# Moving the first attention steps of batch 1 out of the first FFN tile of batch 0

## The chip, the core and the metric

The kernel runs on one core of a Trainium2 chip. The metric is the device time of one execution in microseconds (us). A core has TensorE for matrix products (PE; its weight loads are listed as PEld), VectorE (DVE), ScalarE (ACT), GpSimd (POOL) and SyncE (SP), which here issues the loads and stores. Each engine works through its own list of instructions in order and waits, where an instruction needs something, for the engine or the transfer that makes it.

## The reference

Eight batches, eight heads, 576 rows of q, k and v with 64 columns, and 32 pack rows p. Per batch and head two softmax attentions follow one another; then an FFN with a softplus between its layers.

```
def sm_attn(qq, kk, vv):
    s = scale * matmul(qq, kk.T)
    a = exp(s - max(s)); a = a / (sum(a) + 1e-9)
    return matmul(a, vv)
p_packed = sm_attn(p, k, v)
out = sm_attn(q, p_packed, p_packed)
x = out as (4608, 512)
h = x @ w_in                                   # 512 x 2048
g = maximum(h, 0) + log1p(exp(-abs(h)))
return g @ w_out                               # 2048 x 512
```

## The kernel before

**Tiles and slots.** The FFN runs over units (b, f): 8 batches of 576 rows times 16 tiles of 128 columns of the hidden layer. In the text a tile is one unit, counted within its batch, and `u` is its number over all batches. The second layer of a unit runs LAG = 2 units behind its first, so in unit u PE does, in this order: `gemm1` of u (12 matmuls, six for each of two halves of the 576 rows, into `ph_u_0` and `ph_u_1`), then four slots, t = 0 to 3, with three matmuls each into `acc_t` for unit u - 2, and every so often `make_m`, which prepares the weights of a later tile. All fp32 operands of the FFN are split in a high and a low part (`at_h`/`at_l`, `mh`/`ml`, `gh`/`gl`, `wo_h`/`wo_l`), hence three matmuls for each product.

**Softplus.** ACT takes Abs (L603), Exp (L605) and Ln (L606) of a `ph` pair into `e`; DVE adds max(h, 0) (L608) and splits the result into `gh` and `gl` (L595, L596). `ph` has two banks, so `ph_u_0` of the next tile has to wait for L608 on the half before. POOL keeps the last 64 rows (`rest`, L612).

**Attention folded in.** `make_m` multiplies the packed result `pt` with `w_in` into `psm`, so that the first layer needs only the second softmax (`at`). The attention of batch b + 1 is a generator, `attention_first` for batches 0 and 1. It yields after each of its 30 steps. The order of batch 1's steps on PE is: four transposes of k for head group 0 (`psT_k_0_0` to `psT_k_0_3`, copied by ACT to `T_k` at L269), scores, four transposes of k for group 1 with softmax in between, `psa` (transposed weights) and `psp` (times v, scaled by DVE into `pp` at L327), transposes of q, `psx` (pt), and the second scores and softmax, which end in `aT`. `weights(b + 1)` at the last tile of a batch turns `aT` into `at_h` (ACT, L526) and `at_l` (DVE, L527).

**When a step runs.** In every slot `due` grows by PACE = 0.56 (0.62 while b is 1), and one step is taken for each whole unit of it. `due` starts at 0 at each batch's first tile. So batch 1's first two steps fall into the slots of batch 0's tile 0, and its 30th into tile 13. At tile 15 whatever is left would be run at once; nothing is left.

**Weight conversion.** `w_in` and `w_out` come as 64-bit floats and are converted in 32 pieces by a second generator, `convert`: ACT makes `m` and `r` (L200, L204), DVE `t` (L206, L211), POOL adds them into `w_in_sb` or `r` (L219), and for `w_out` ACT and DVE split the sum (L238, L244). Most of it runs in batch 0's slots, at CONV = 1.6 steps for each slot. In batch 0 a `psm` pair serves two tiles and needs the columns of two pieces of `w_in`; it stands at the end of the slots two tiles ahead. So the last two pieces are needed ahead of tile 13, by the `psm` for tiles 14 and 15.

**Banks.** Everything of the attention and `psm` share two PSUM banks (`ps_m`, taken in turn). A tile that takes a bank waits until the reader of the tile before the last is done.

**Order.** PE's instructions run in the order of the code. The order on ACT, DVE, POOL and SP is set when the kernel is built, by a list scheduler that goes by priority and by what it takes to be ready; so moving a step in the code can also reorder the conversion and the softplus on these engines.

Of the kernel before, what the change touches and what calls it, by code (L numbers as in the profile page):

```python
# [26 lines left out]
def pack_attention_then_softplus_ffn(  # L27
# [27 lines left out]
    FIRST = 2  # L55
# [39 lines left out]
    def load_pack(bg, queues):  # L95

        t = cv.tile([PW, H, D], F32, tag="m", name=f"p_{bg}", bufs=1)
        for i in range(BG):
            queues[i % len(queues)].dma_start(
                t[i * J:(i + 1) * J], p[bg * BG + i].rearrange("h j d -> j h d")  # L100
            )
        return t

    def pack_transposed(bg, t):
        for o in range(0, H, HG):
            ps = bank(f"ppt_{bg}_{o}")
            for i in range(HG):
                nc.tensor.transpose(
                    ps[:D, i * PW:(i + 1) * PW], t[:, o + i, :], ident[:PW, :PW]
                )  # L110
            dst = pT[:, o:o + HG, :].rearrange("x h j -> x (h j)")
            nc.vector.tensor_copy(dst[:D], ps[:D, :HG * PW])
            nc.scalar.copy(dst[D:], ps[:D, :HG * PW])
# [402 lines left out]
    def attention(b):  # L516
        return attention_first(b) if b < FIRST else attention_next(b)

    def weights(b):

        at_h = work.tile([P, G, S], F32R, tag="at_h", name=f"at_h_{b}", bufs=1)
        at_l = work.tile([P, G, S], F32R, tag="at_l", name=f"at_l_{b}", bufs=1)
        res[b]["at"] = (at_h, at_l)
        for g in range(G):
            aT = res[b]["aT"][g]
            nc.scalar.copy(at_h[:, g, :], aT)  # L526
            nc.vector.tensor_tensor(  # L527
                at_l[:, g, :], aT, at_h[:, g, :].bitcast(F32), op=ALU.subtract
            )


    def m_cols(b):

        return MC if b else MC // 2
# [30 lines left out]
    def gemm1(b, f, res):  # L565

        n = m_cols(b)
        halves = res["m"][f * P // n]
        at_h, at_l = res["at"]
        phs = []  # L570
        for c in range(2):
            ph = ps_h.tile([P, 512], F32, tag="h", name=f"ph_{b}_{f}_{c}")
            phs.append(ph[:, :C])
            i = 0
            for g in range(G):
                mh, ml = halves[g * n // MC]
                o = g * n % MC + f * P % n
                ms = slice(o, o + P)
                cs = slice(c * C, (c + 1) * C)
                for x, y in ((mh, at_h), (mh, at_l), (ml, at_h)):  # L580
                    nc.tensor.matmul(  # L581
                        ph[:, :C], x[:, ms], y[:, g, cs],
                        start=(i == 0), stop=(i == 3 * G - 1),
                    )
                    i += 1
        return phs
# [11 lines left out]
    def softplus(b, f, hv, done):  # L598
        e = work.tile([P, S], F32, tag="e", name=f"e_{b}_{f}")
        es = [e[:, c * C:(c + 1) * C] for c in range(2)]  # L600
        spans = [e] if b == 0 else es
        for c in range(2):
            nc.scalar.activation(es[c], hv[c], AF.Abs)  # L603
            for x in spans[c:c + 1] if b else spans[:c]:
                nc.scalar.activation(x, x, AF.Exp, scale=-1.0)  # L605
                nc.scalar.activation(x, x, AF.Ln, bias=1.0)  # L606
        for c in range(2):
            nc.vector.scalar_tensor_tensor(es[c], hv[c], 0.0, es[c], op0=ALU.max, op1=ALU.add)  # L608
        yield
        yield  # L610
        r = (b % 2) * REST
        nc.gpsimd.tensor_copy(rest[:, rest_at(b, f), r:r + REST], e[:, NT * P:])  # L612
        yield
        done[b, f] = halves(f"{b}_{f}")
        split(*done[b, f], e[:, :NT * P])

    def gemm2_tile(acc, gh, gl, f, cs, first, last):
        for i, (x, y) in enumerate(((gh, wo_h), (gh, wo_l), (gl, wo_h))):
            nc.tensor.matmul(  # L619
                acc, x[:, cs], y[:, f, :],  # L620
                start=(first and i == 0), stop=(last and i == 2),
            )
# [13 lines left out]
    def store(acc, pieces, nm, t):  # L636
        if t % 2 == 0:
            half[:] = [cv.tile([P, 2, DM], F32, tag="x", name=f"o_{nm}", bufs=2)]
        o = half[0][:, t % 2, :]
        nc.vector.tensor_copy(o, acc)  # L640
        for row, b, col, n in pieces:
            while n:
                m, dst = rows(b, col, n)
                nc.sync.dma_start(dst, o[row:row + m, :])
                row, col, n = row + m, col + m, n - m

    def rests(b):


        fs = sorted(range(NF), key=lambda x: rest_at(b, x))  # L650
        gh, gl = halves(f"{b}_m")
        n = NT // 2
        for i in range(0, NF, n):
            o = rest_at(b, fs[i])
            c = i % NT * P
            cs = slice(c, c + n * P)
            split(gh[:, cs], gl[:, cs], rest[:, o:o + n, :].rearrange("x f j -> x (f j)"))
            if i == 0:
                yield
                am = ps_acc.tile([P, DM], F32, tag="acc", name=f"acc_{b}_m")  # L660
            for t in range(n):
                gemm2_tile(
                    am, gh, gl, fs[i + t], slice(c + t * P, c + (t + 1) * P),
                    i + t == 0, i + t == NF - 1,
                )
        store(am, [(0, b - 1, NT * P, REST), (REST, b, NT * P, REST)], f"{b}_m", NT)
        yield
# [7 lines left out]
    PACE = 0.56  # L675
    FRONT = 1000
    PACE_FIRST = 0.62
# [18 lines left out]
    due = 0.0  # L696
# [20 lines left out]
    ahead, chain, due = iter(()), iter(()), 0.0  # L717
    for u in range(len(units) + LAG):
        if u < len(units):
            b, f = units[u]  # L720
            if f == 0:
                if (b + 1) % BG == 0 and b + 1 < B:
                    pack_transposed((b + 1) // BG, pt)
                ahead = attention(b + 1) if b + 1 < B else iter(())
                due = 0.0
            chain = softplus(b, f, gemm1(b, f, res[b]), gs)
            next(chain)
            if f == NF - 1:
                if (b + 2) % BG == 0 and b + 2 < B:
                    pt = load_pack((b + 2) // BG, (nc.sync,))  # L730
                for _ in ahead:
                    pass
                if b + 1 < B:
                    weights(b + 1)
        if u >= LAG:
            b2, f2 = units[u - LAG]
            gh, gl = gs.pop((b2, f2))
            if f2 == 0:
                acc = [ps_acc.tile([P, DM], F32, tag="acc", name=f"acc_{b2}_{t}") for t in range(NT)]
        last = u >= LAG and f2 == NF - 1 and b2 % 2 == 1  # L740
        if last:
            both = rests(b2)
            next(both)
        for t in range(NT):
            if u >= LAG:
                gemm2_tile(
                    acc[t], gh, gl, f2, slice(t * P, (t + 1) * P), f2 == 0, f2 == NF - 1
                )
                if f2 == NF - 1:
                    store(acc[t], [(0, b2, t * P, P)], f"{b2}_{t}", t)  # L750
            if u < len(units):
                due += PACE if b != FIRST - 1 else PACE_FIRST
                while due >= 1:
                    next(ahead, None)
                    due -= 1
                if b == 0:
                    cdue += CONV
                    while cdue >= 1:
                        next(conv, None)
                        cdue -= 1  # L760
            next(chain, None)
        if last:
            next(both)
        if u + 2 < len(units):


            nb, c = units[u + 2][0], units[u + 2][1] * P
            if c % m_cols(nb) == 0:
                make_m(nb, c // m_cols(nb), res[nb])
# [29 lines left out]
```

## Time and profile before

| | |
|---|---|
| median of 3 runs | 772.29 us (771.9 to 772.75) |
| the profiled execution | 772.78 us |
| its span, first to last instruction | 771.0 us |
| mean granted clock of PE | 0.973 |
| busy PE / DVE / ACT / POOL | 733.0 / 527.6 / 434.8 / 99.1 us |
| start of batch 0's first `ph` | 39.16 us |
| start of batch 1's first `ph` | 151.55 us |

A row of the timeline has the start in us, the duration in us, the engine, the line, the operation, out<-in, the shape and the count of instructions merged in it; in brackets stands how long the engine sat idle before it and what ended that. The granted clock is the share of full speed that PE was given in a stretch. A row of the waits has the total in us, the number of times and the longest.

### The profile page before, as it was taken

What the parts mean: (1) busy time and instruction counts of PE and PEld (TensorE: products, weight loads), DVE (VectorE), ACT (ScalarE), POOL (GpSimd) and SP (SyncE); (2) the same over time, 40 slices, a digit from 0 to 9 for tenths busy, and PEclk for the clock granted to TensorE, in tenths of its full rate; (3) what the DMA queues carried; (4) which work ended last, traced back from release to release, by engine and by line L of the source; (5) the groups of instructions that cost most, each with busy time, mean ns of one, the idle gap of its engine ahead of it and who ended that gap; (6) DMA issues with size and microseconds to landing.
All of it is one profiled execution on the core that took longest, in us unless ns stands there. A gap on an engine that the chain in (4) does not pass through costs nothing.

```text
span 771.0 us, 14168 instructions
## 1 busy us (share of the span) xinstructions
PE 733.0 (95%) x5360; PEld 579.5 (75%) x5360; DVE 527.6 (68%) x1092; ACT 434.8 (56%) x1057; POOL 99.1 (13%) x166
## 2 busy tenths in 40 slices
PE   6657998999999999999999999999999999999997
PEld 3445775887787778878788777878787777888886
DVE  2697879965877569565967559575867558565554
ACT  5668877766454545565555455565555355555540
POOL 1143444200000000000000000000010000000110
PEclk9559999999999999999999999999999999999999
DMA  9978655434403341052302342052402400010002
GB/s 211 237 185 190 185 137 150 95 76 73 93 1 76 56 81 44 1 124 47 79 1 76 55 64 61 1 109 42 91 2 61 70 1 1 1 55 1 1 1 68
DMA packets 149668, 55.97 MB, mean 73 GB/s; under 512 B 116320, under 2 KB 142944, under 8 KB 149600
## 3 DMA queue, kind: packets, MB, share of 16 engines
q1 hardware_dynamic: 149328, 55.00, 31.9%
q8 instruction: 42, 0.69, 0.4%
q14 instruction: 26, 0.21, 0.1%
q10 hardware_dynamic: 272, 0.07, 0.0%
HBM read 45.61 MB, written 9.44 MB: 71 GB/s over the span
## 4 chain that ended last, share of the span: by engine, by line
PE 85%; DVE 6%; ACT 4%; DMA 3%; issue 1%; POOL 1%; SPq 0%; ACTq 0%; DVEq 0%; POOLq 0%
PE acc L619 42%; PE ph L581 26%; PE acc_m L619 6%; PE psm L544 4%; PE ps L276 2%; DMA w_in_sb<-in_q 2%; PE psp L319 2%; PE psa L309 1%; DVE at_l L527 1%; DVE e L608 1%; DVE t L206 1%; ACT e L605 1%; DVE t L211 1%; ACT e L603 1%; DMA k<-in_k 1%
## 5 line engine op out<-in xcount | busy, mean ns | idle before, releaser
L603 ACT ACTIVATE e<-ph 128x288 f32<-128x288 f32 x256 | 103.2, 404 | 190.4 <-PE ph L581 143.4
L619 PE MATMUL acc<-wo_h,gh 128*128 128x512 f32 x512 | 208.0, 406 | 0.0
L608 DVE SCALAR_TENSOR_TENSOR e<-ph,e 128x288 f32<-128x288 f32 x256 | 113.4, 451 | 132.4 <-ACT e L606 131.3
L619 PE MATMUL acc<-wo_l,gh 128*128 128x512 f32 x512 | 201.2, 393 | 0.0
L619 PE MATMUL acc<-wo_h,gl 128*128 128x512 f32 x512 | 201.0, 393 | 0.0
L581 PE MATMUL ph<-at_h,mh 128*128 128x288 f32 x512 | 159.0, 311 | 12.7 <-ACT at_h L526 6.6
L581 PE MATMUL ph<-at_l,mh 128*128 128x288 f32 x512 | 153.6, 300 | 3.7 <-DVE at_l L527 3.7
L581 PE MATMUL ph<-at_h,ml 128*128 128x288 f32 x512 | 152.9, 299 | 0.0
L581 PEld LDWEIGHTS ph<-at_h,mh 128*128 128x128 f32 x512 | 97.9, 191 | 46.7 <-DVE gl L596 9.6
L612 POOL COPY rest<-e 128x64 f32<-128x64 f32 x128 | 53.8, 420 | 577.3 <-DVE e L608 547.7
L619 PEld LDWEIGHTS acc<-wo_h,gh 128*128 128x128 f32 x512 | 96.4, 188 | 27.5 <-issue 10.2
L619 PEld LDWEIGHTS acc<-wo_h,gl 128*128 128x128 f32 x512 | 96.3, 188 | 21.1
L605 ACT ACTIVATE e<-e 128x288 f32<-128x288 f32 (+1 forms) x240 | 109.4, 456 | 4.0
L606 ACT ACTIVATE e<-e 128x288 f32<-128x288 f32 (+1 forms) x240 | 109.4, 456 | 3.2
L619 PEld LDWEIGHTS acc<-wo_l,gh 128*128 128x128 f32 x512 | 96.6, 189 | 13.1
L581 PEld LDWEIGHTS ph<-at_l,mh 128*128 128x128 f32 x512 | 98.1, 192 | 8.1 <-DVE at_l L527 5.3
L581 PEld LDWEIGHTS ph<-at_h,ml 128*128 128x128 f32 x512 | 98.1, 192 | 0.0
L596 DVE TENSOR_TENSOR gl<-e,gh 128x512 fp32r<-128x512 f32 x128 | 87.7, 685 | 5.5
L559 ACT CAST mh<-psm 128x512 fp32r<-128x512 f32 (+1 forms) x72 | 35.9, 539 | 54.5 <-PE psm L544 54.3
L595 DVE CAST gh<-e 128x512 fp32r<-128x512 f32 x128 | 55.5, 434 | 5.5 <-DVE e L608 0.5
L560 DVE TENSOR_TENSOR ml<-psm,mh 128x512 fp32r<-128x512 f32 (+1 forms) x72 | 42.8, 623 | 20.6 <-ACT mh L559 20.0
L544 PE MATMUL psm<-w_in_sb,pt 64*32 64x512 f32 (+1 forms) x576 | 41.3, 567 | 7.6 <-ACT T_k L269 4.8
(79 smaller groups left out, 696.4 us busy)
## 6 DMA issues: line engine op xcount, KB each, us to landing
v<-in_v SPq DMA_DIRECT2D x16, 576.0 KB, 4.9
x_i<-in_moe_w_in SPq DMA_DIRECT2D x28, 256.0 KB, 4.4
k<-in_k SPq DMA_DIRECT2D x48, 144.0 KB, 3.2
q<-in_q SPq DMA_DIRECT2D x48, 144.0 KB, 3.1
x_o<-in_moe_w_out SPq DMA_DIRECT2D x11, 512.0 KB, 3.8
out<-o SPq DMA_DIRECT2D x18, 256.0 KB, 2.5
rest<-in_moe_w_out SPq DMA_DIRECT2D x5, 512.0 KB, 6.1
k<-in_k SPq DMA_DIRECT2D x4, 576.0 KB, 6.7
```

Source lines behind the costliest of these rows:

```text
L544: nc.tensor.matmul(ps[hh * J:(hh + 1) * J, :n], res["pt"][g][o:o + D, hh * J:(hh + 1) * J], w_in_sb[o:o + D, hh, c * n:(c + 1) * n], start ...
L559: nc.scalar.copy(mh[:, cols], ps[:, :n])
L560: nc.vector.tensor_tensor(ml[:, cols], ps[:, :n], mh[:, cols].bitcast(F32), op=ALU.subtract)
L581: nc.tensor.matmul(ph[:, :C], x[:, ms], y[:, g, cs], start=(i == 0), stop=(i == 3 * G - 1),)
L595: nc.vector.tensor_copy(hi, x)
L596: nc.vector.tensor_tensor(lo, x, hi.bitcast(F32), op=ALU.subtract)
L603: nc.scalar.activation(es[c], hv[c], AF.Abs)
L605: nc.scalar.activation(x, x, AF.Exp, scale=-1.0)
L606: nc.scalar.activation(x, x, AF.Ln, bias=1.0)
L608: nc.vector.scalar_tensor_tensor(es[c], hv[c], 0.0, es[c], op0=ALU.max, op1=ALU.add)
L612: nc.gpsimd.tensor_copy(rest[:, rest_at(b, f), r:r + REST], e[:, NT * P:])
L619: nc.tensor.matmul(acc, x[:, cs], y[:, f, :], start=(first and i == 0), stop=(last and i == 2),)
```

## The change

In the slots of u = 0 `due` no longer grows. From u = 1 on it grows as before.

```
             if u < len(units):
-                due += PACE if b != FIRST - 1 else PACE_FIRST
+                due += (PACE if b != FIRST - 1 else PACE_FIRST) if u >= 1 else 0
                 while due >= 1:
                     next(ahead, None)
                     due -= 1
```

Every step of batch 1's attention is taken four slots later, the 30th in tile 14 in place of tile 13. The attention of the other batches is where it was, and so is the conversion, whose steps are taken by a count of their own.

On PE, between tile 0's `ph` and tile 2's, the rows before are these, with `psT_k` the transposes of k, `psm` the tile's later weights and `ph_1` tile 1's first layer:

```order
L263 MATMUL psT_k_0_0_551<-ident,k_0_497 128x96 x3
L263 MATMUL psT_k_0_1_573<-ident,k_0_497 128x96 x3
L544 MATMUL psm_1_0_587<-w_in_sb,pt_0_351 32x256 x4
L544 MATMUL psm_1_1_588<-w_in_sb,pt_1_428 32x256 x4
L581 MATMUL ph_1_0_603<-at_h_521,mh_0_0_515 128x288
```

And after, in the same place, up to the first row of `ph_1` and then from its last row on:

```order
L544 MATMUL psm_1_0_573<-w_in_sb,pt_0_351 32x256 x4
L544 MATMUL psm_1_1_574<-w_in_sb,pt_1_428 32x256 x4
L581 MATMUL ph_1_0_589<-at_h_521,mh_0_0_515 128x288
...
L581 MATMUL ph_1_1_596<-at_h_521,ml_0_0_516 128x288
L263 MATMUL psT_k_0_0_622<-ident,k_0_497 128x96 x3
L263 MATMUL psT_k_0_1_637<-ident,k_0_497 128x96 x3
```

The two transposes no longer stand between tile 0's `ph` and `psm`, but behind tile 1's `ph`.

On ACT, in the softplus of tile 4 (`e_4`), the rows before, with `T_k_1_x` the copies of group 1's transposes and `m`, `r`, `wo_h` of the conversion:

```order
L603 ACTIVATE e_4_851<-ph_4_0_837 128x288
L238 CAST wo_h<-t_809 128x512
L603 ACTIVATE e_4_851<-ph_4_1_844 128x288
L605 ACTIVATE e_4_851<-e_4_851 128x576
L269 COPY T_k_1_3_865<-psT_k_1_3_861 128x288
L606 ACTIVATE e_4_851<-e_4_851 128x576
```

And after:

```order
L603 ACTIVATE e_4_834<-ph_4_0_820 128x288
L296 ACTIVATE a_1_0_620,z_1_0_844<-a_1_0_620,nm_1_0_801 128x576
L200 ACTIVATE m_719<-x_o_618 128x512
L204 ACTIVATE r_789<-x_o_649 128x512
L603 ACTIVATE e_4_834<-ph_4_1_827 128x288
L269 COPY T_k_1_1_850<-psT_k_1_1_846 128x288
L605 ACTIVATE e_4_834<-e_4_834 128x576
L200 ACTIVATE m_787<-x_o_649 128x512
L238 CAST wo_h<-t_723 128x512
L606 ACTIVATE e_4_834<-e_4_834 128x576
L269 COPY T_k_1_2_875<-psT_k_1_2_871 128x288
```

Tile 4's softplus now has the first softmax's Exp (L296) and more of the conversion within it, and the copies of the second and third transposes in place of that of the fourth.

On DVE, at the last piece of `w_in` (`t_1518` before, `t_1491` after, each made from an `m` of ACT), the rows before, with `e_12` the softplus of tile 12:

```order
L255 STREAM_TRANSPOSE k_0_1834<-k_0_1834 128x576 x2
L608 SCALAR_TENSOR_TENSOR e_12_1564<-ph_12_0_1550,e_12_1564 128x288
L206 TENSOR_SCALAR t_1518<-m_1514 128x512
L608 SCALAR_TENSOR_TENSOR e_12_1564<-ph_12_1_1557,e_12_1564 128x288
L211 SCALAR_TENSOR_TENSOR t_1518<-m_1514,t_1518 128x512
```

And after, with `e_11` the softplus of tile 11:

```order
L608 SCALAR_TENSOR_TENSOR e_11_1476<-ph_11_1_1469,e_11_1476 128x288
L206 TENSOR_SCALAR t_1491<-m_1487 128x512
L595 CAST gh_11_1524<-e_11_1476 128x512
L211 SCALAR_TENSOR_TENSOR t_1491<-m_1487,t_1491 128x512
L596 TENSOR_TENSOR gl_11_1525<-e_11_1476,gh_11_1524 128x512
```

The piece is one tile earlier among the softplus tiles, though its conversion step is taken in the same slot of the code.

More of the change, by code (lines that the diff above doesn't have):

```diff
@@ L751, in pack_attention_then_softplus_ffn @@
             if u < len(units):
-                due += PACE if b != FIRST - 1 else PACE_FIRST
+                due += (PACE if b != FIRST - 1 else PACE_FIRST) if u >= 1 else 0
                 while due >= 1:
```

## The prediction

> **What bounds the kernel now.** I read the page first, then the busy time in stretches cut at tile starts, then the waits, and then the timelines of the engines in batch 0.
>
> ```profile
> span 771.0 us, 14168 instructions
> ...
> PE 733.0 (95%) x5360; PEld 579.5 (75%) x5360; DVE 527.6 (68%) x1092; ACT 434.8 (56%) x1057; POOL 99.1 (13%) x166
> ```
>
> ```profile
> 46.30:54.40 8.10, 3.32 (x24) 1.35 (x23) 6.90 (x12) 5.89 (x12) 4.72 (x4) 0.50 0.59 166
> 68.50:75.50 7.00, 5.21 (x38) 4.24 (x30) 4.87 (x13) 7.00 (x17) 3.29 (x3) 1.00 0.84 220
> 75.50:83.10 7.60, 7.57 (x62) 4.90 (x62) 7.60 (x14) 6.41 (x16) 3.52 (x5) 1.00 0.92 229
> 83.10:88.90 5.80, 5.80 (x80) 4.82 (x76) 4.65 (x12) 5.80 (x14) 3.49 (x3) 1.00 0.51 156
> 134.90:140.70 5.80, 5.80 (x29) 5.17 (x25) 4.93 (x10) 4.58 (x10) 1.57 (x1) 0.71 0.25 39
> 160.00:200.00 40.00, 40.00 (x360) 30.39 (x359) 24.83 (x55) 22.49 (x58) 2.63 (x8) 1.00 0.44 81
> ```
>
> After each stretch's length come the busy times of PE, PEld, DVE, ACT and POOL, then the granted clock. From 160 us on PE is busy all the time at full clock: there only less PE work would help, and the change alters none. Batch 0's FFN (39 to 151 us) is another matter. In tile 0 (46.3 to 54.4) PE works 3.32 of 8.1 us at half clock; in tiles 3 to 5 ACT is busy 7.00 of 7.0, 6.41 of 7.6 and 5.80 of 5.8 us, because the weight conversion runs beside the FFN. So whatever PE gains there it must also get past ACT.
>
> ```profile
> 46.33 1.16 PE L263 MATMUL psT_k<-ident,k 96*128 96x96 f32 x6
> 50.28 1.08 PE L544 MATMUL psm<-w_in_sb,pt 64*32 64x256 f32 x8 [2.79 <-ACT T_k L269]
> 54.36 0.61 PE L581 MATMUL ph<-at_h,mh 128*128 128x288 f32 x1
> 60.95 0.61 PE L581 MATMUL ph<-at_h,mh 128*128 128x288 f32 x1 [3.05 <-DVE e L608]
> 75.53 0.40 PE L581 MATMUL ph<-at_h,mh 128*128 128x288 f32 x1 [1.81 <-DVE e L608]
> 83.10 0.40 PE L581 MATMUL ph<-at_h,mh 128*128 128x288 f32 x1
> 95.40 0.40 PE L581 MATMUL ph<-at_h,mh 128*128 128x288 f32 x1
> 134.27 0.67 PE L544 MATMUL psm<-w_in_sb,pt 64*32 64x256 f32 x16 [1.65 <-POOL w_in_sb L219]
> 134.87 0.40 PE L581 MATMUL ph<-at_h,mh 128*128 128x288 f32 x1
> 140.88 0.30 PE L581 MATMUL ph<-at_h,mh 128*128 128x288 f32 x1
> 151.55 0.40 PE L581 MATMUL ph<-at_h,mh 128*128 128x288 f32 x1
> 156.01 0.29 PE L581 MATMUL ph<-at_h,mh 128*128 128x288 f32 x1
> ```
>
> ```profile
> PE ph L581 <- DVE e L608: 6.0, 4, 3.1
> PE psm L544 <- ACT T_k L269: 4.8, 2, 2.8
> ```
>
> These are the first matmuls of tiles 1, 2, 4, 5, 7, 13, 14, of batch 1's tiles 0 and 1, and the `psm` groups ahead of tiles 1 and 13. What stands in brackets is the wait. In batch 0 PE loses 4.8 us because `psm` needs the two banks that the transposed k fills just before, 6.0 us for the softplus of the tile before, and 1.65 us for the last weight columns.
>
> **The change part by part.** No instruction is added or removed; every step of batch 1's attention moves four slots back. From batch 1's tile 0 on (151.55) the order of PE is the old one, so the whole effect is how much earlier that matmul starts. I carried the new order forward by hand from 46.33, each instruction starting when its engine is free and its inputs and banks are, with the spacings of these rows:
>
> ```profile
> 49.18 0.68 ACT L606 ACTIVATE e<-e 128x576 f32<-128x576 f32 x1
> 85.42 0.70 ACT L200 ACTIVATE m<-x_o 128x512 f32<-128x512 f32 x1
> 85.97 0.73 ACT L605 ACTIVATE e<-e 128x576 f32<-128x576 f32 x1
> 88.24 0.62 ACT L238 CAST wo_h<-t 128x512 fp32r<-128x512 f32 x1
> 88.76 0.67 ACT L200 ACTIVATE m<-x_o 128x512 f32<-128x512 f32 x1
> ```
>
> ```profile
> 51.62 0.81 DVE L608 SCALAR_TENSOR_TENSOR e<-ph,e 128x288 f32<-128x288 f32 x2
> 90.49 0.68 DVE L596 TENSOR_TENSOR gl<-e,gh 128x512 fp32r<-128x512 f32 x1
> 91.09 0.27 DVE L327 TENSOR_SCALAR pp<-psp,rs 128x64 f32<-128x64 f32 x1
> 91.28 0.68 DVE L211 SCALAR_TENSOR_TENSOR t<-m,t 128x512 int32<-128x512 int32 x1
> ```
>
> On ACT the conversion's `m` takes 0.55 us from start to start (85.42 to 85.97) and the `wo_h` cast 0.52 (88.24 to 88.76); on DVE `gl` takes 0.60 and one half of `pp` 0.19.
>
> *Tile 0.* The first `psm` follows tile 0's `ph` at once, without the 2.79 us wait, from 46.33 to about 48.4 (twice 1.08 at half clock). What is late next is tile 0's softplus, whose rows ahead of it are the old ones: its last DVE step starts at 51.62 and the first half ends near 52.05. Tile 1 starts there, not at 54.36: 2.3 us. Its second `ph` half ends near 55.1 (12 matmuls at 0.24 us from start to start, as before at half clock). ACT then runs Abs, Exp, one conversion step and Ln (0.4 + 0.6 + 0.55 + 0.6) to near 57.4, DVE follows, and tile 2 starts near 57.85 instead of 60.95: 3.1 us.
>
> *Tiles 2 to 4.* With the scores one tile later, tile 3's softplus ends near 69.8 and tile 4 starts near 70.35, not at 75.53. At tile 5 (83.10 before) the copy of the third k transpose stands behind tile 4's Ln on ACT. From the end of tile 3's Ln (69.8) ACT has 15 instructions up to and with that Ln, six of them `m` and `r` of 0.55 us, together 7.4 us, so that it ends near 77.2; and the `psm` ahead of tile 5 needs its bank: a new wait of 1.9 us. Tile 5 starts near 77.85, a lead of 5.25 us, part of which is attention work only put off.
>
> *Tiles 5 and 6* give most of it back. The fourth k transpose waits about 0.95 us for `ml`, the scores another 0.7 for the copy behind tile 5's Ln; and the second `psm` ahead of tile 7 needs the bank of `psp`, which DVE now reads behind `gl` of tile 6: from the end of tile 6's softplus (90.7) come `wo_l`, `t`, `gh`, `t`, `gl` and two halves of `pp`, 0.6 + 0.35 + 0.35 + 0.6 + 0.6 + 0.4 = 2.9 us, to near 93.6. PE is there at 91.35: 2.25 us. Tile 7 starts near 94.25 instead of 95.40. Lead 1.15.
>
> *Tiles 7 to 12* regain some: by the same carrying, the waits for softplus shrink and 0.85 us of scores stands one tile later, and the lead at the `psm` ahead of tile 13 is about 3.85.
>
> *The last weight columns.*
>
> ```profile
> 130.64 0.67 ACT L200 ACTIVATE m<-x_i 128x512 f32<-128x512 f32 x1
> 131.44 0.40 DVE L206 TENSOR_SCALAR t<-m 128x512 int32<-128x512 int32 x1
> 132.13 0.67 DVE L211 SCALAR_TENSOR_TENSOR t<-m,t 128x512 int32<-128x512 int32 x1
> 132.95 1.27 POOL L219 TENSOR_TENSOR w_in_sb<-t,r 128x512 int32<-128x512 int32 x1
> ```
>
> Before, this piece goes through ACT and DVE in tile 12's softplus and leaves POOL at 134.2, when PE has waited 1.65 us. In the new order it stands behind tile 11's softplus on both engines; I get POOL done near 127 and PE there near 128.6. The wait goes, with 1.6 us of cover. So does what follows it: tile 13, 12 `ph` and 12 `acc` matmuls, takes 6.01 us (134.87 to 140.88) at clock 0.71, the same 24 in batch 1's tile 0 4.46 us (151.55 to 156.01): 1.55 us. Lead 5.5 at tile 13.
>
> *The end of batch 0.*
>
> ```profile
> 145.52 0.76 DVE L368 STREAM_TRANSPOSE aT<-a 128x576 f32<-128x576 f32 x1
> 149.67 0.66 ACT L526 CAST at_h<-aT 128x576 fp32r<-128x576 f32 x1
> ```
>
> The last `aT` is there 3.4 us before its reader today; one tile later about 0.9 us are left. I cost it at nothing, since `at_h` must wait for tile 15's `ph` anyway; without the 0.9, each microsecond late is one lost. Adding the 1.55 and taking off 1.15 for scores and small waits done in tile 13, the lead at batch 1's first matmul is 5.9 us.
>
> *Queues.*
>
> ```profile
> q<-in_q SPq DMA_DIRECT2D x48, 144.0 KB, 3.1
> ...
> 69.33 0.38 SPq L127 DMA_DIRECT2D q<-in_q  x1
> ...
> 91.28 0.41 PE L263 MATMUL psT_q<-ident,q 96*128 96x96 f32 x3
> ```
>
> On SP the q loads move behind weight loads: one issued at 69.33 today lands 3.1 us later and is read first at 91.28. That is 19 us of cover, and its reader moves back by a tile too; without it, its landing would be waited for, 3.1 us. POOL runs no attention step. Both cost nothing.
>
> *The unknown: the clock after a new wait.* The 1.65 us wait at 134.27 was followed by half clock, the 1.81 us one at 75.53 by full clock. So a wait of this size costs between 0 and 1.55 us more; the two new ones of 1.9 and 2.25 us could each do it. One in two did, and part would fall into the next wait: I charge half a window, 0.8 us. [...]
>
> **Sum:** 5.9 − 0.8 = 5.1 us. The profiled execution took 772.78 us (span 771.0, 1.8 us around it, left as it is), 0.49 above the median of the runs shown. From that median, 772.29 − 5.1 = 767.2 us.
>
> **The rivals.**
> A. *The lead of the front is kept.* If the order of ACT and DVE leaves no wait in tiles 4 to 6, the 4.1 us lost between tiles 5 and 7 (5.25 − 1.15) stay: 763.1 us. For it: DVE has 1.15 us free in tile 5 (4.65 of 5.8). Against it: ACT's rows above.
> B. *Taken back entirely.* ACT is the bound from tile 3 to 6, and the attention steps only shift: nothing is left of the front; only 1.65 + 1.55 remain: 769.1 us.
> C. *The last columns come no earlier relative to PE either*: 772.3 us. It needs the conversion held up by over 1.6 us, its load from HBM for instance.
> D. *Slower: the clock.* The new order has five waits of about 1 us or more where PE is now at full clock (ahead of tile 2, ahead of tile 5, in tile 5, ahead of tile 7, and near 117 us for a bank). If each brings one half-clock window, 5 × 1.55 = 7.75 us stand against 5.9: 774.1 us. The fourth such window turns the gain into a loss. Against it: the wait at 75.53 brought none.
> That the change does something else is no rival: PE's order shows exactly four slots.
>
> **How the numbers follow.** Forecast 0.42, A 0.15, B 0.20, C 0.12, D 0.11. Faster than 770.7 (0.2%, about what a measurement of this kernel can tell from no change) are the forecast, A and B: 0.77; C is the same, 0.12; D slower, 0.11. The range reaches below A, to the ceiling of 5.9 + 4.1 us at 762.3, and above C, to 772.8; it leaves out D and the edges of A and C.
>
> **What would show it.** Right: no wait of `psm` for T_k ahead of tile 1; tile 2 near 57.9 us; no wait for POOL ahead of tile 13 and full clock in it; batch 1's first matmul near 146. Wrong: tile 7 later than 95.4, clock below 1.0 in tiles 5 to 10, or `at_l` named as the releaser of batch 1's first matmuls.

## The result, and the profile after

The changed kernel takes 779.11 us, the median of 6 runs (777.97 to 782.7); the kernel before, beside it, 772.52 us, the median of 6 (771.9 to 774.54). The ratio is 1.0085, with a 95% interval of 1.0061 to 1.011: 6.6 us slower, where 5.1 us of gain were forecast. The profiled execution took 778.41 us (span 776.6, against 771.0).

The page of the changed kernel, its head: the instructions that matter are the same in number, and PE's busy time differs by 1.7 us only.

```profile
span 776.6 us, 14177 instructions
...
PE 734.7 (95%) x5360; PEld 579.9 (75%) x5360; DVE 528.4 (68%) x1092; ACT 434.8 (56%) x1057; POOL 97.8 (13%) x166
```

Starts of the tiles (their first `ph` matmul, from the timelines; 16 is batch 1's tile 0), in us:

| tile | 1 | 2 | 4 | 5 | 6 | 7 | 9 | 10 | 12 | 13 | 16 |
|---|---|---|---|---|---|---|---|---|---|---|---|
| before | 54.36 | 60.95 | 75.53 | 83.10 | 88.87 | 95.40 | 108.31 | 113.80 | 126.85 | 134.87 | 151.55 |
| after | 51.74 | 57.82 | 69.81 | 78.43 | 89.76 | 98.93 | 111.06 | 120.32 | 133.85 | 139.96 | 156.93 |
| lead | 2.6 | 3.1 | 5.7 | 4.7 | -0.9 | -3.5 | -2.8 | -6.5 | -7.0 | -5.1 | -5.4 |

Tile 0's first `ph` stands at 39.16 us before and at 38.77 after, ahead of anything that the change moves; so 0.4 us of each lead up to tile 5 is not the change's. Up to tile 4 the change does what was worked out. Between tiles 4 and 7 it gives back 9.2 us, and between 7 and 12 another 3.5. From tile 12 to 16 the lead grows by 1.6 us, and from tile 16 on nothing changes.

The timeline of PE in the changed kernel, its rows with waits (in brackets the wait and its releaser):

```profile
51.74 0.61 PE L581 MATMUL ph<-at_h,mh 128*128 128x288 f32 x1 [4.57 <-DVE e L608]
57.82 0.40 PE L581 MATMUL ph<-at_h,mh 128*128 128x288 f32 x1 [1.43 <-DVE e L608]
...
77.58 0.64 PE L544 MATMUL psm<-w_in_sb,pt 64*32 64x256 f32 x8 [1.78 <-ACT T_k L269]
...
83.43 0.74 PE L263 MATMUL psT_k<-ident,k 96*128 96x96 f32 x3 [1.31 <-DVE ml L560]
...
98.37 0.64 PE L544 MATMUL psm<-w_in_sb,pt 64*32 64x256 f32 x8 [2.31 <-DVE pp L327]
...
115.23 0.47 PE L263 MATMUL psT_q<-ident,q 96*128 96x96 f32 x3 [1.60 <-DVE ml L560]
...
156.93 0.40 PE L581 MATMUL ph<-at_h,mh 128*128 128x288 f32 x1 [0.42 <-DVE e L608]
```

The waits at 77.58, 83.43 and 98.37 are the three forecast (1.9, 0.95 and 2.25 us), within 0.4 us of their sizes; the one at 115.23 had been seen but not priced. What follows each of them is the news. The same kernel in stretches (length, then busy PE, PEld, DVE, ACT, POOL, then the granted clock):

```profile
76.07:79.48 3.41, 1.68 (x16) 1.20 (x17) 3.19 (x7) 3.41 (x9) 2.02 (x3) 1.00 1.05 239
79.48:89.72 10.24, 8.93 (x40) 5.71 (x39) 8.74 (x16) 6.35 (x14) 3.93 (x5) 0.50 0.49 150
96.55:99.96 3.41, 1.59 (x15) 1.21 (x16) 3.38 (x8) 1.60 (x3) 1.28 (x1) 1.00 0.81 210
99.96:103.38 3.42, 3.42 (x14) 2.96 (x13) 1.87 (x4) 2.76 (x6) 1.97 (x2) 0.50 0.41 150
113.62:117.03 3.41, 1.81 (x55) 1.40 (x54) 3.19 (x6) 2.18 (x5) 0.67 (x1) 1.00 0.23 93
117.03:120.44 3.41, 3.41 (x26) 2.58 (x14) 2.59 (x6) 0.26 (x1) 1.66 (x2) 0.50 0.63 172
```

Behind each of three stretches of 3.41 us in which PE worked under 1.9 us, the clock is halved, in whole multiples of 3.41 us: three after the first, one after each of the others. PE was busy in 8.93 + 3.42 + 3.41 = 15.8 us of these; at full clock the same work would take about 7.9 us less, if half the clock is twice the time: an estimate, from `ph` matmuls of the kernel before that follow one another at 0.24 us at half clock (136.18 to 136.42) and at 0.13 at full (141.01 to 141.14). How much of that would have come back is another matter, since PE might then have waited for the other engines (e14 below). The kernel before has only one such stretch of 3.41 us behind tile 3, at 135.5.

An account of the loss: over 38 to 175 us (summed over windows of 0.5 us) PE is idle 17.8 us before and 19.8 after, and busy at half clock 16.4 and 24.5. 2.0 us of idle time and 8.1 / 2 = 4.05 us of half clock make 6.05 us, against 5.6 us of span. This is bookkeeping: PE's work is the same, so a loss has to show as idle time or as half clock. It says where the time stands, not what a cure of either would give back.

### The profile page after: what moved, and what is told of

Its sections match the earlier page's. It is cut to its first block, busy times and chain, and to the rows that moved or that the text cites. A ratio compares the mean times of both kernels' runs of the same rounds, so it can differ in the third digit from the quotient of the medians.

```text
span 776.6 us, 14177 instructions
## 1 busy us (share of the span) xinstructions
PE 734.7 (95%) x5360; PEld 579.9 (75%) x5360; DVE 528.4 (68%) x1092; ACT 434.8 (56%) x1057; POOL 97.8 (13%) x166
## 4 chain that ended last, share of the span: by engine, by line
PE 84%; DVE 6%; ACT 4%; DMA 3%; issue 1%; POOL 1%; SPq 0%; ACTq 0%; POOLq 0%; DVEq 0%
PE acc L619 42%; PE ph L581 25%; PE acc_m L619 6%; PE psm L544 4%; PE ps L276 3%; DMA rest<-in_moe_w_out 2%; PE psp L319 1%; DVE at_l L527 1%; PE psa L309 1%; DMA x_i<-in_moe_w_in 1%; DVE wo_l L244 1%; ACT e L605 1%; ACT m L200 1%; ACT e L603 1%; DVE t L206 1%
## 5 line engine op out<-in xcount | busy, mean ns | idle before, releaser
L596 DVE TENSOR_TENSOR gl<-e,gh 128x512 fp32r<-128x512 f32 x128 | 89.7, 701 | 5.9 <-DVE z L363 0.3
L560 DVE TENSOR_TENSOR ml<-psm,mh 128x512 fp32r<-128x512 f32 (+1 forms) x72 | 42.6, 621 | 19.8 <-ACT mh L559 19.2
L544 PE MATMUL psm<-w_in_sb,pt 64*32 64x512 f32 (+1 forms) x576 | 39.4, 560 | 5.4 <-ACT T_k L269 2.5
```

What stands on the lines that cost most here:

```text
L544: nc.tensor.matmul(ps[hh * J:(hh + 1) * J, :n], res["pt"][g][o:o + D, hh * J:(hh + 1) * J], w_in_sb[o:o + D, hh, c * n:(c + 1) * n], start ...
L560: nc.vector.tensor_tensor(ml[:, cols], ps[:, :n], mh[:, cols].bitcast(F32), op=ALU.subtract)
L596: nc.vector.tensor_tensor(lo, x, hi.bitcast(F32), op=ALU.subtract)
```

## The experiments

Four theories stood against each other in turn. *Clock*: the moved steps make waits in tiles 4 to 9, each halves PE's clock, and that is the loss. *Queue*: ScalarE and VectorE set when tiles 6 to 12 can start, whatever PE does. *Reorder*: the scheduler places the weight conversions anew on the other engines when a step moves, and that costs. *Fit*: steps and conversions are matched so closely that any move or delay costs. Times are medians; "before" is the kernel before in the same runs, and ratios are to it, unless the text says otherwise. The diffs show only the lines that matter. `keep_busy` issues the given number of dummy matmuls of 128 x 224, whose results nobody reads.

**e1, withheld in tile 0, caught up in tile 1** (against the changed kernel):

```diff
-                due += (PACE if b != FIRST - 1 else PACE_FIRST) if u >= 1 else 0
-                while due >= 1:
+                due += PACE if b != FIRST - 1 else PACE_FIRST
+                while due >= 1 and u >= 1:
```

> Batch 1's first two steps are withheld in tile 0 and caught up in the first slot of tile 1; from tile 2 on the attention is where it was before the change. Clock theory (the change loses its time because the shifted steps make waits of 1.6 to 2.3 us for banks in tiles 4 to 9, and each lets the clock fall to half for a window of about 3.4 us, some 1.6 us of PE time): those waits are not there, half clock after tile 2 stays at one window or none, and the lead of the front, about 2 us at tile 2, is kept: 768 to 771 us. Queue theory (ACT and DVE set the time of batch 0 in tiles 3 to 10, whatever the clock does): the lead is eaten by the softplus of tile 3, 772 us as before, within 1 us.

774.24 us, ratio 1.0019 (1.0008 to 1.003), 1.1 us above before (773.16) and outside what both theories expected, though nearer to the queue theory. Tile 4 starts at 71.68, 3.9 us ahead of before (1.3 of these because this execution's tile 0 starts at 37.83), yet tile 5 at 83.33: a new wait and a half-clock stretch (79.4 to 82.8) take the whole lead.

```profile
78.33 0.70 PE L276 MATMUL ps<-T_k,pT 64*32 64x288 f32 x10 [2.51 <-ACT T_k L269]
```

**e2, one wait filled with dummy matmuls**, and **e3, the copy that ends it put first**, both against the changed kernel:

```diff
+            if g == 0:
+                keep_busy(ps, FILL_M.get((b, c), 0), 256)     # e2: 14 at (0, 3)
```

```diff
+                    if u in (4,):                             # e3
+                        with tc.high_priority(offset=60):
+                            next(ahead, None)
```

> The changed kernel with 14 extra matmuls (128 x 224, results unused) between the two psm groups ahead of tile 5, where PE waits 1.78 us for the copy of T_k; they take about 1.4 us, so PE starts tile 5 no later. Clock theory: the clock stays at 1.00 in tile 5 (it was 0.50 from 79.8 to 89.6 us), tile 6 starts 3 to 5 us earlier, and the time falls to 774 to 776 us. Queue theory: the clock stays up, but tile 6 waits for the softplus of tile 5 and for the scores' banks instead, and the time stays at 778 to 780 us.

> The changed kernel with the attention steps of tile 4 given priority, so that ACT copies T_k of the third transpose ahead of tile 4's Exp instead of behind its Ln; nothing else is asked for. The wait of 1.78 us ahead of tile 5 should go. Clock theory: the clock stays full in tile 5 and 3 to 5 us come back, 774 to 776 us. Queue theory: tile 4's softplus ends as much later as the copies and what else moves ahead of it take (about 1 us), tile 5 waits for L608 in place of T_k, and the time stays at 778 to 780 us.

778.45 us (ratio 1.0069, 1.0049 to 1.0089) and 779.19 us (1.0069, 1.0047 to 1.009). In both the wait left its place and came back at another:

```profile
85.33 0.74 PE L265 MATMUL psT_k<-ident,k 96*128 96x96 f32 x3 [3.15 <-DVE ml L570]
```

```profile
81.44 0.61 PE L581 MATMUL ph<-at_h,mh 128*128 128x288 f32 x1 [3.76 <-DVE e L608]
```

The first row is e2's, the second e3's. Tile 6 starts at 91.73 and 88.72. Both times lie where the queue theory had them.

**e4, twelve artificial waits of graded length in batches 2 to 7** (the kernel before; GpSimd copies a piece of the tile's `gh` several times, and a transpose on PE reads the last copy):

```diff
+            if (b, f) in LADDER:
...
+                for i in range(LADDER[b, f]):
+                    nc.gpsimd.tensor_copy(sc[:, 1 - i % 2, :], sc[:, i % 2, :])
+                nc.tensor.transpose(ph_now[0][:64, C:C + P], sc[:, LADDER[b, f] % 2, :], ident)
```

> The kernel before, with one artificial PE wait of graded length ahead of tiles 5 and 11 of batches 2 to 7 (twelve in all): POOL copies a 128 x 64 piece 2 to 12 times after the tile's gh, and a PE transpose reads the last copy. In these batches PE has no waits and runs at full clock. Clock theory: waits under about 1 us leave the clock at 1.00; from about 1.7 us on (half of a window of 3.4 us) a window at 0.50 follows, in some cases at the length where the wait straddles a window's edge it does not; each such window costs about 1.6 us beyond the wait. Queue theory says nothing of the clock; if no wait up to 3 us lowers it, the clock theory falls.

826.1 us, one execution. Three of the rows (0.92, 2.12 and 3.61 us):

```profile
359.45 0.30 PE L775 MATMUL ph<-ident,sc 128*64 128x128 f32 x1 [0.92 <-POOL sc L774]
551.82 0.30 PE L775 MATMUL ph<-ident,sc 128*64 128x128 f32 x1 [2.12 <-POOL sc L774]
394.26 0.42 PE L775 MATMUL ph<-ident,sc 128*64 128x128 f32 x1 [3.61 <-POOL sc L774]
```

The three waits up to 1.52 us were followed by full clock, the five from 2.12 to 2.88 us by one stretch of 3.41 us at half, the four from 3.61 us on by 6.83 us of it. The clock does fall behind the nine waits from 2.12 us on, as the clock theory has it; what that costs in batch 0 is not shown by it.

**e5, all new waits filled; e6 and e7, nine of VectorE's `wo_l` subtractions left out after and before; e8, the conversion at 1.7 steps a slot in the kernel before:**

```diff
+    FILL_M = {(0, 1): 16, (0, 3): 14, (0, 4): 18}             # e5
+    FILL_S = {(5, 0): 8, (9, 0): 12}
```

```diff
-            if w == "o":                                      # e6, e7
+            if w == "o" and i not in range(3, 12):
```

```diff
-    CONV = 1.6                                                # e8
+    CONV = 1.7
```

e6 and e7 let the second layer read `wo_h` in place of the `wo_l` that they leave out, so their result is not that of the reference.

> The changed kernel with short dummy matmuls (N = 224, 68 in all) ahead of each of the places in batch 0 at which its profile shows TensorE waiting longest (psm_1, psm_3, psm_4, psT_k_1_3, psT_q_0_1), so that TensorE is busy there instead of idle. Clock theory: the half-clock stretches from 79.8 to 120 us go, with them (20.2 - 12.5) / 2 = 3.9 us or most of it, the waits themselves stay: 774 to 775.5 us, granted clock 0.98 or more. Queue theory (ScalarE's and VectorE's order sets when tile 6 and the later tiles can start): other waits take their place, tile 6 still starts at 89 to 92 us, 778 to 780 us.

> The changed kernel without VectorE's subtraction that makes wo_l for weight columns 3 to 11 (the second GEMM reads wo_h in its place for these columns, so TensorE's work is the same): 9 VectorE instructions fewer in the slots of about tiles 3 to 12, nothing else. Queue theory: these instructions stand in the row that sets tiles 4 to 9, so tile 6 starts 1.5 us or more earlier than 89.8 us and the time falls by 2.5 us or more, to 776.5 us or less. Clock theory: the waits at psm and at psT_k are ended by one or two instructions that stand elsewhere; less than 1 us of gain, 778 to 779.5 us, the half-clock stretches stay at three or more.

> The kernel before with the same part left out (wo_l of columns 3 to 11). With e6 it tells whether VectorE's load is what makes the shift cost time. Queue theory: the kernel before gains less than the changed one, and the difference between the two (6.6 us) shrinks to under 3 us: 770 to 772 us. Clock theory: the difference stays at 5 us or more; 771.5 to 773 us here.

> The kernel before with the weight conversion's pace at 1.7 steps a slot in place of 1.6: the last w_in column comes earlier, which takes away the wait of 1.65 us ahead of tile 13 and the half-clock stretch of 3.4 us behind it. Clock theory: 772.5 - 1.65 - 1.5 = 769.4 us, 768.5 to 770.5. Queue theory: the conversions stand earlier in the queues of ScalarE and VectorE in tiles 2 to 10, and take there what the last wait gives back: 772 to 774 us.

799.21, 780.92, 777.59 and 778.69 us: each above the kernel it was made from (e5 and e6 from the changed one; e6's 1.8 us lie within the intervals), and outside what either theory expected. Leaving out VectorE work cost the kernel before 4.4 us (ratio 1.0058, 1.0041 to 1.0075). A likely reason shows in the order of the instructions, and it reaches back to e1 to e3: TensorE alone runs in the written order; on the other engines the scheduler lets a small edit move the conversions' `m`, `r`, `t`, `wo_h` and `wo_l` past the FFN's `e`, `gh`, `gl` and `ml`. Of ScalarE's some 260 instructions ahead of 175 us, compared by name in the traces, 20 and 25 stand elsewhere in e2 and e3, 78 to 209 in e1 and e5 to e8, and 1 in e4. So e1 to e3 and e5 to e8 each change more than their diffs show; e4 does not. e5 has a flaw besides, told at e9.

**e9 to e14, e16 and e17 hold that order.** After tracing, ordering edges without semaphores fix the rows of ScalarE, VectorE, GpSimd and the DMA queue to the one named (`m` FFN, `c` conversion, `a` attention steps). In e10 and e11 only `m` and `c` are fixed, and the scheduler still places the attention steps among them:

```diff
+    for engine, text in PINNED.items():
+        row = [keys[engine, t[0], int(t[1:])] for t in text.split()]
+        for x, y in zip(row, row[1:]):
+            tc.add_manual_dep(y, x.name, no_sync, reason="as before")
```

**e9, the changed kernel, own order held, three waits filled; e10, the steps moved, the conversions in the order of before; e11, the reverse.**

> The changed kernel with 51 dummy matmuls (N = 224) ahead of psm_3_1 (15), psT_k_1_3 (18) and psm_4_1 (18), with the order of all instructions on ScalarE, VectorE, GpSimd and the DMA queue held to the changed kernel's own (in e2 and e5 the scheduler was free to reorder around the dummies). So the one thing that differs is that TensorE is busy where it waited 1.78, 1.31 and 2.31 us. Clock theory: the half-clock stretches of 79.8 to 89.6 and 100 to 103.4 us go; TensorE was busy in about 11 us of these 13.7, so up to 5.5 us come back, less what the waits then take: 774 to 776.5 us. Queue theory: tile 6 still starts at 89 us or later since ScalarE and VectorE end what it waits for, 778 to 780 us.

> The changed kernel with the conversions' and the FFN's instructions on ScalarE, VectorE, GpSimd and the DMA queue held in the relative order that they have in the kernel before; the attention steps alone move. The scheduler reorders the conversions when any step moves: in the changed kernel they stand elsewhere among the FFN's instructions than before. Reorder theory (it is this reordering that costs the time, not the later steps): 768 to 773 us. Clock and queue theories (the later steps cost it): 777 to 780 us.

> The counterpart: the kernel before, its attention steps where they are, with the conversions' and the FFN's instructions on ScalarE, VectorE, GpSimd and the DMA queue held in the relative order that they have in the changed kernel. Reorder theory: 776 to 780 us. Clock and queue theories: 772 to 774 us, as before within 0.2%.

e9: 781.05 us, and it tells nothing: its dummies ahead of psT_k_1_3 wrote into a bank that VectorE had yet to read, and waited themselves (so did e5's):

```profile
88.50 4.18 PE L550 MATMUL ph<-wo_h 128*128 128x224 f32 x18 [4.08 <-DVE e L631]
```

e10: 782.57 us (ratio 1.0128, 1.0113 to 1.0143). e11: 779.57 us (1.0091, 1.0071 to 1.0111). In e11 TensorE's order is that of before, and it loses as much as the change, as the reorder theory had it; in e10 the steps move and conversions and FFN keep their order, and it loses more, above what every theory expected. So the two halves of the change do not add up (9.9 and 6.9 us against 6.6 together), and the loss belongs to neither alone. Since the attention steps' places on ScalarE and VectorE are new in both, the two do not part the causes cleanly. e10's longest new wait, and the two of e11 that a half-clock stretch follows:

```profile
98.85 1.08 PE L554 MATMUL psm<-w_in_sb,pt 64*32 64x256 f32 x8 [4.56 <-DVE pp L337]
```

```profile
82.62 0.91 PE L554 MATMUL psm<-w_in_sb,pt 64*32 64x256 f32 x16 [1.56 <-ACT a L295]
...
127.44 0.40 PE L591 MATMUL ph<-at_h,mh 128*128 128x288 f32 x1 [2.85 <-DVE e L618]
```

The first is e10's, the others e11's.

**e12, one artificial wait between psm_3_0 and psm_3_1 of the kernel before; e13, the same place with PE busy** (order of before held; the copies on GpSimd are in both):

```diff
+            if (b, c, g) == (0, 3, 0):
+                nc.tensor.transpose(ps[:64, n:n + P], sc[:, 0, :], ident)
+                for i in range(7):
+                    x = nc.gpsimd.tensor_copy(sc[:, i % 2, :], sc[:, 1 - i % 2, :])
+                nc.tensor.transpose(ps[:64, n:n + P], sc[:, 0, :], ident)   # e12
+                for i in range(20):                                         # e13
+                    nc.tensor.matmul(ps[:, n:n + 224], wo_h[:, 0, :P], wo_h[:, 0, :224], ...)
```

> The kernel before, order on the four other engines held to its own, with one artificial wait of TensorE of about 2.3 us between psm_3_0 and psm_3_1 (a transpose of a small tile, seven copies of it on GpSimd, a transpose of the result). It prices one wait with its half-clock window in a stretch where the kernel before has TensorE busy throughout. Clock theory: the wait and half of one 3.41 us window, 772.7 + 2.3 + 1.6 = 776.6 us, and 1.2 to 2.2 us above e13. Fit theory (the queues of the four engines are matched to each other so closely that any delay of one grows): 777 us or more, and e13 within 0.8 us of it.

> The same, but TensorE spends that time in 20 dummy matmuls (N = 224, about 2.2 us at full clock) instead of waiting; the copies on GpSimd stay. Clock theory: the delay alone, 772.7 + 2.2 = 774.9 us, 774 to 775.5. Fit theory: 776.5 us or more, a delay of 2.2 us that costs 4 us.

e12: 777.79 us (ratio 1.0074, 1.0061 to 1.0087). e13: 774.28 us (1.0036, 1.0021 to 1.005). The wait came out at 3.26 us, with two half-clock stretches behind it (84.2 to 91.1), where e13 has none:

```profile
85.32 0.42 PE L567 MATMUL psm<-ident,sc 128*64 128x128 f32 x1 [3.26 <-POOL sc L565]
```

The second `psm` ahead of tile 5 and two stretches around and behind it (a row of the timeline, then two of the stretches), first in e12, then in e13:

```profile
85.68 1.08 PE L556 MATMUL psm<-w_in_sb,pt 64*32 64x256 f32 x8
84.24:87.65 3.41, 2.33 (x13) 1.30 (x14) 1.31 (x4) 1.77 (x4) 0.84 (x4) 0.50 0.03 5
87.65:91.07 3.42, 3.42 (x14) 3.13 (x14) 0.64 (x3) 2.09 (x5) 1.28 (x1) 0.50 0.47 153
```

```profile
85.53 0.64 PE L556 MATMUL psm<-w_in_sb,pt 64*32 64x256 f32 x8
84.92:88.33 3.41, 3.41 (x30) 2.79 (x29) 1.91 (x5) 2.69 (x7) 1.80 (x7) 1.00 0.08 13
88.33:91.75 3.42, 3.42 (x58) 2.57 (x60) 2.11 (x6) 3.42 (x8) 1.75 (x2) 1.00 0.65 217
```

From tile 4 to tile 6 the kernel before takes 13.34 us, e13 15.78 and e12 19.54. Of the 3.76 us between the two, about 1.45 lie ahead of this `psm`: the longer wait. The other 2.3 lie behind it: from there to tile 6 e13 takes 6.40 us (85.53 to 91.93) and e12 8.69 (85.68 to 94.37), with the same instructions in the same order and no wait in either. This is the price of the clock: what runs behind the wait is the same in both. A delay of 2.4 us with PE busy costs 2.25 us in the end: it does not grow, and the fit theory falls in this point.

**e14, the changed kernel, own order held, dummies at psm_3_1 (15) and psm_4_1 (18) only:**

> e9 without the dummies ahead of psT_k_1_3: these lay in a bank that VectorE still had to read, so that they themselves made TensorE wait 4.1 us. The changed kernel, order held, with dummy matmuls at psm_3_1 (15) and psm_4_1 (18) alone. Clock theory: three to four of the five half-clock windows behind tile 4 go, 775 to 777 us. Queue and fit theories: TensorE then waits longer at psT_k_1_3 for VectorE's ml, over 2 us, which brings the half clock back there; 778 to 780 us.

777.07 us (ratio 1.0066, 1.0052 to 1.0079): 1.5 us better than the changed kernel by the ratios, 2.0 by the medians, though the intervals overlap. Of the five stretches behind tile 4 two are left (85.7 and 116.5); the first is that of a wait that only moved:

```profile
85.63 0.68 PE L275 MATMUL psT_k<-ident,k 96*128 96x96 f32 x3 [2.42 <-DVE ml L580]
```

Tile 4 to tile 6 still takes 18.63 us (19.95 in the changed kernel, 13.34 before): of what the filling frees, part goes into a longer wait for VectorE (2.42 us, 1.31 in the changed kernel), as the queue theory has it. The half clock that goes is worth some 2.4 us by the account above (19.6 us busy at half clock instead of 24.5), the gain 1.5 to 2.0.

**e15, the steps two slots earlier; e18, two slots later** (both against the kernel before, order free):

```diff
-                due = 0.0
+                due = 0.0 if b else 2 * PACE                                    # e15
```

```diff
-                due += PACE if b != FIRST - 1 else PACE_FIRST
+                due += (PACE if b != FIRST - 1 else PACE_FIRST) if 4 * u + t >= 2 else 0   # e18
```

> The kernel before with batch 1's attention begun two slots (half a tile) earlier, the opposite of the change (due starts at 1.12 in batch 0 instead of 0). Fit theory: slower too, by 2 to 8 us (774.5 to 781), since any shift breaks the match of steps and conversions. Clock and queue theories, by which later steps are what costs: the same or faster, 770 to 773.5 us.

> The change at half its size: batch 1's attention begins two slots later instead of four. Fit theory (any move breaks the match of steps and conversions): 2 to 8 us above the kernel before, 774.5 to 781, with no need to lie between the two. If the cost grows with how late the steps are: half of 6.6 us, 775 to 776.5 us. If only the four-slot shift puts the banks' releases behind the wrong instructions: 772 to 773.5 us.

e15: 778.82 us (ratio 1.0088, 1.0073 to 1.0104). e18: 784.61 us (1.0141, 1.0114 to 1.0168). Two slots earlier cost as much as four later, as the fit theory expected and the clock and queue theories did not; two later cost nearly twice that (12.5 us by the medians, 10.9 by the ratio), more than every theory expected. It is no matter of later or earlier. e18 shows the clock plainest: between 84 and 153 us its profiled execution, the slowest of five (780.52 to 787.59 us), spends 23.9 us at half clock, 23.0 of them busy:

```profile
84.12:90.94 6.82, 6.33 (x26) 5.04 (x27) 4.14 (x11) 4.55 (x12) 2.44 (x2) 0.50 0.18 45
114.84:121.66 6.82, 6.59 (x26) 5.15 (x27) 4.15 (x8) 4.21 (x8) 3.03 (x2) 0.50 0.56 169
131.90:138.72 6.82, 6.64 (x28) 5.32 (x29) 6.59 (x11) 4.23 (x10) 2.56 (x2) 0.50 0.75 193
148.96:152.38 3.42, 3.42 (x17) 3.21 (x14) 3.42 (x7) 0.78 (x2) 0.00 (x0) 0.50 0.86 191
```

The five executions are one program, and their times go with the mean granted clock: 780.5 and 781.9 us at 0.977 and 0.976, 784.6 and 785.7 at 0.962, 787.6 at 0.953.

**e16, the kernel before, order held, dummies in both of its waits that a half-clock stretch follows; e17, in the second alone:**

```diff
+            if u == 2:                                        # e16 only
+                spot = ps_acc.tile([P, 512], F32, tag="acc", name="spot")
+                keep_busy(spot, 26, 0)
...
+        if (b, c) == (0, 7):
+            keep_busy(pss[0], 15, 256)
```

> The kernel before, order on the four other engines held to its own, with dummy matmuls (N = 224) in its two remaining waits with a half-clock window behind them: 26 ahead of tile 2's first ph (3.05 us, window 60 to 64) and 15 ahead of psm_7 before tile 13 (1.65 us, window 135.5 to 139). Clock theory: TensorE was busy for some 3.2 us of each window, so half of that twice, 3.2 us less than before: 769.2 us, 768.3 to 770.5, faster than both kernels. Queue and fit theories: the next waits for VectorE and GpSimd take it back, 771.5 to 773 us.

> The same with the second of the two alone (15 dummies ahead of psm_7). Clock theory: 1.6 us less than before, 770.8 us. Queue and fit theories: 772 to 773 us.

e16: 772.06 us against 773.09, ratio 0.9985 (0.9972 to 0.9998), faster than both kernels by a narrow margin, 1.0 us, a third of what was expected. e17: 772.71 us, 0.9999 (0.9988 to 1.001), the same; so holding the order costs nothing by itself that shows here. The stretch at 135 us is gone from both profiles and the one at 60 from e16's, as planned; in the profile of each another has come, behind tile 4's old wait of 1.8 us. These profiles are not the best executions: five of e16's twelve, at a mean granted clock of 0.983 to 0.985, took 769.8 to 771.3 us, and the seven at 0.976 to 0.981, the profiled one among them, 772.0 to 773.9. In the kernel before that wait falls across two windows of 3.41 us, in e16 into one (first row before, then e16):

```profile
74.07:77.49 3.42, 1.96 (x14) 1.92 (x15) 3.06 (x7) 2.80 (x7) 1.67 (x3) 1.00 1.13 223
```

```profile
72.87:76.28 3.41, 1.58 (x12) 1.44 (x11) 3.00 (x7) 3.12 (x7) 1.73 (x3) 1.00 1.12 226
76.28:79.70 3.42, 3.42 (x13) 2.54 (x11) 3.25 (x4) 2.65 (x7) 1.59 (x1) 0.50 0.98 246
```

The account over 38 to 175 us, each against the kernel before (idle 17.8, busy at half clock 16.4): what idle time and half clock make together is the loss of span within about 1 us, where no dummies fill PE (in e3 and e6 to e8, left out of the table, within 0.8 us). The two terms share the loss differently from run to run: half clock is the larger in the changed kernel, e1, e12 and e18, idle time in e10, e11 and e15.

| run | idle | busy at half | more idle + half of more at half | span more by |
|---|---|---|---|---|
| changed kernel | 19.8 | 24.5 | 2.0 + 4.05 | 5.6 |
| e1 | 17.5 | 18.8 | -0.3 + 1.2 | 1.4 |
| e10 | 25.3 | 23.4 | 7.5 + 3.5 | 9.9 |
| e11 | 21.9 | 20.7 | 4.1 + 2.15 | 5.9 |
| e12 | 19.5 | 20.3 | 1.7 + 1.95 | 3.9 |
| e15 | 20.6 | 19.4 | 2.8 + 1.5 | 4.4 |
| e18 | 21.4 | 40.0 | 3.6 + 11.8 | 14.8 |

So no theory holds alone. Clock: seen behind nine of e4's twelve waits, and priced at 2.3 us behind e12's wait (against e13), but filling waits gave back no more than 2 of the changed kernel's 6.6 us (e14), and e15's loss is mostly idle time. Queue: right in the times of e2 and e3, with waits that only move. Reorder: right in e11, wrong in e10. Fit: right in e15, wrong in e13, too low in e18.

## Why the prediction was wrong

- *Tile 0 and tiles 2 to 4*: right, within 0.6 us and with the waits where they were expected. Tile 1 at 51.74 (52.05 worked out), tile 2 at 57.82 (57.85), tile 4 at 69.81 (70.35), tile 5 at 78.43 (77.85), the wait ahead of it 1.78 us (1.9). The start of tile 0, 0.4 us earlier, is in these.
- *The unknown: the clock after a new wait*: **the step that failed**. It charged the new waits half a window, 0.8 us (half of the 1.55 us read at tile 13). Behind them stand five stretches of half clock with 7.9 us more than at full clock; over the whole of batch 0 it is 4.05 us more than before, mainly since the stretches at 60 and 135 us of the kernel before are gone. The prediction counted one of two waits; the trace before has a third, the 3.05 us ahead of tile 2, and half clock follows it too (60.42 to 63.83). It took "one in two did" for a chance between 0 and 1.55 us for all waits together, where it is one for each wait. In tile 5 three stretches at half clock follow one another: the wait of 1.31 us that ends at 83.43 lies 0.77 us in the first (79.48 to 82.89) and 0.54 in the second. That it kept the clock low is an estimate from these times; no run shows it by itself. Rival D had the mechanism, the waits ahead of tile 5, in tile 5, ahead of tile 7 and near 117, and the price, 7.75 us against the 7.9 above; only the wait ahead of tile 2 stayed harmless. Its chance of 0.11 was too low. D's time of 774.1 us still lies 5.0 us below the measured 779.11, since D kept the lead of 5.9 us.
- *That lead* did not hold either. It ends at -5.4 us, 11.3 below the 5.9 worked out: 0.6 of this had gone by tile 5, 4.1 go between tiles 5 and 7, 6.2 between 7 and 12, 0.4 behind them. At most 7.9 of the 11.3 is the half clock of the five stretches; e14, where three of the five were gone, gave back 1.5 to 2.0 us.
- *Tiles 5 and 6*: the waits for `ml` and `pp` right (1.31, 2.31; 0.95 and 2.25 worked out), the further 0.7 for the scores not in the trace, the sum wrong. From tile 5 to tile 7 the kernel before takes 12.30 us, the changed one 20.50: 8.2 us given back, not 4.1. In 79.48 to 89.72 PE's 8.93 us of work at half clock are up to 4.5 of that.
- *Tiles 7 to 12 regain some*: wrong. 2.7 us of gain were carried forward; the stretch takes 34.92 us instead of 31.45, a loss of 3.5. The two half-clock stretches in it (99.96 and 117.03) account for up to 3.4; of the gain itself the wait of 1.60 us at 115.23, seen but not priced, took a part. Where the rest went is not shown.
- *The last weight columns*: right. No wait for POOL ahead of tile 13 and full clock in it; from tile 12 to tile 16 the lead grows by 1.6 us, where 2.05 (1.65 + 1.55 - 1.15) was worked out.
- *Queues* and *the end of batch 0*: nothing in the waits speaks against them.

What stays open: why the order of before has so few waits from tile 4 to 12, and whether an order exists that keeps the front's lead. Also open is how the loss divides between the steps, the new order on the other engines and the clock: each was seen to cost time, and no run parts them in the changed kernel. Every other order of steps and conversions that ran was slower, by 1.1 us (e1) to 12.5 us (e18) by the medians; that this holds for all orders is not shown. In the changed kernel's own order two fills gave back 1.5 to 2 us (e14). A kernel in which the clock stayed full throughout was not had.

## What to carry to other kernels

Price a new wait of TensorE, where it is otherwise busy, at its own length plus the clock it loses behind it (2.3 us behind e12's wait of 3.26), and do that for every wait; in the changed kernel the second part was the larger (4.05 us against 2.0). Where a scheduler orders the other engines, hold that order before reading an experiment: an edit that looks like one change moved the conversions on three engines, and such a new order, with TensorE's own order as before, cost 6.9 us (e11). An early lead of one engine is safe only if the next stage can keep it: here 5.7 us at tile 4 were gone at tile 6.

## What the runs showed of the hardware

Fourteen profiled executions (before, after, e1, e4, e8 and e10 to e18) were cut, from 41 to 44 us on up to 763 to 766 us (816 in e4), into stretches of 3.413 us, each execution from a start of its own. All 2974 stretches show a granted clock of 1.00 or of 0.50, none a value between. The length stands in the kernel before: from 63.83, where the clock returns to full, to 135.51, where it halves, it is 71.68 us, 21 times 3.413. The changes of the clock stand at 2.39 us plus multiples of 3.413 before, at 0.97 after, at 1.19 in e16; e4's profile has 23 of them. The wait of 1.8 us ahead of tile 4 has full clock behind it before, where two stretches share it (0.35 and 1.46 us of idle PE), and half clock in e16, where it lies in one (1.83 us).

Of these stretches 2845 at full clock have another behind them. With 1.9 us or more of idle PE all 27 were followed by half clock; with 1.5 to 1.9 us 11 of 15 (not the 1.89 us from 120.97 on in e15); with less 4 of 2803 (the least 1.11 us, from 107.24 on in e8). All 56 returns from half to full clock came after stretches with at most 0.69 us of idle time; but 33 stretches at half clock with 0.16 to 1.28 us of it were followed by another at half. These are counts in this case's executions; what decided where they differ is not shown.
